# Products with the values issued three chunks at a time in a fused attention, experts and feed-forward kernel

## The chip, the cores and the metric

The kernel runs on one core of a Trainium2 chip. Its time is the device time of one execution in microseconds (us); three runs of the kernel before took 1173.31, 1173.35 and 1174.44 us, the median is 1173.35 us. The engines are TensorE (PE in the profile, its weight loads PEld), VectorE (DVE), ScalarE (ACT), GpSimd (POOL) and SyncE (SP), which here issues the transfers. Each engine works through its own instructions in their order, and waits at an instruction until the semaphores it names have come.

## The reference

The input passes three layers: attention whose queries are averaged in pairs, a mixture of eight experts of which each token takes one, and a dense feed-forward layer with softplus. All is float32. Only the attention is touched by the change in its order:

```python
def _attn_ref(q, k, v):                     # 4 batches, 8 heads, 1152 tokens, 64 wide
    q_pool = q.reshape(B, H, S // factor, factor, D).mean(axis=3)     # 576 queries
    scores = scale * np.matmul(q_pool, k.transpose(0, 1, 3, 2))
    scores = scores - np.max(scores, axis=-1, keepdims=True)
    attn = np.exp(scores)
    attn = attn / (np.sum(attn, axis=-1, keepdims=True) + 1e-09)
    return np.matmul(attn, v).astype(np.float32)
...
        h = np.maximum(x[mask] @ w1[e], 0.0)                 # experts, 512 -> 1024 -> 512
        out[mask] = gate_w[mask, None] * (h @ w2[e])
...
    h = x @ w_in                                             # 512 -> 2048 -> 512
    g = np.maximum(h, 0.0) + np.log1p(np.exp(-np.abs(h)))
    return (g @ w_out).astype(np.float32)
```

## The kernel before

The attention walks through 16 pairs of heads. A pair has two halves of 288 queries, a half has nine chunks of 128 keys, so there are 288 steps, numbered g; a step treats one chunk of keys for both heads of the pair. What one step issues stands in the loop of line 427:

- `smat(g+1)` (lines 163 to 169): the scores of the next chunk, keys on the partitions, four fp16 matmuls of 288 columns into one of two PSUM tiles `st`. The second of each two carries the low halves of the numbers and the row maximum, which was found earlier.
- `ex(g+1)` (line 170): ScalarE makes the exponentials of that chunk, float32, into a tile `P` (a ring of five buffers).
- `row` (line 421, `srow` in line 109): the scores are also computed the other way round, queries on the partitions, 384 keys at a time, only so that VectorE can take their maximum (line 121). That is done for a later pair, 27 rows a pair, and each row takes one of three PSUM tiles `sr`. `rows(g)` (line 334) says how many rows are to have been issued by step g: mostly five in three steps, and fewer for some twenty steps after each half batch, when VectorE has the routing of the experts to do.
- the events of the step (`ev`): loads, casts, the sums of the exponentials (`rsum`, line 188, in every ninth step), the routing (`lstage`, line 217). Many of these take an `sr` tile too. In a step rows and events take turns.
- `pv(g)` (line 207): the product of the exponentials of this chunk with the values, float32, one matmul for each head, 64 columns of weights each, the two side by side in the array and added up over the nine chunks in one PSUM tile `pv`. Each becomes two passes, so a `pv` is four records of line 212 in the trace.
- `add(g)` (line 174): GpSimd adds up the exponentials over groups of three chunks, for the sums.

At the end of a half `evac` copies the `pv` tile out on ScalarE. After the last step `tail` finishes the routing, then `moe_ffn` runs the experts and the feed-forward layer. The weights of the latter come as float64 words and are converted to float32 by VectorE (`convert`, line 981): twelve chunks during the attention, twenty during the experts. All 32 float32 chunks `W32` have a place in the pool `ws` from the start (line 934), 64 KB in each partition, and the fp16 low halves `wl` are written later into the same slots, each into that of the chunk before it (tags in lines 737 and 934).

The order on every engine is the order in which this code calls the instructions; no scheduler moves them.

Of the kernel before, what the change touches and what calls it, by code (L numbers as in the profile page):

```python
# [9 lines left out]
F32=mybir.dt.float32; F32R=mybir.dt.float32r; F16=mybir.dt.float16; I32=mybir.dt.int32; U32=mybir.dt.uint32  # L10
# [6 lines left out]
def attention(ctx,late,tc,I,C,x_dram,LG,gate,fill,early):  # L17
# [8 lines left out]
    rkp=late.enter_context(tc.tile_pool(name="rk",bufs=2,**R_))  # L26
    qsp=late.enter_context(tc.tile_pool(name="qs",bufs=1,**R_))
    vp=[late.enter_context(tc.tile_pool(name="v0",bufs=1,**R_)),ctx.enter_context(tc.tile_pool(name="v1",bufs=1))]
    pp=ctx.enter_context(tc.tile_pool(name="P",bufs=5))
    accp=ctx.enter_context(tc.tile_pool(name="acc",bufs=4)); ssp=ctx.enter_context(tc.tile_pool(name="ss",bufs=7))  # L30
    xup=ctx.enter_context(tc.tile_pool(name="xu",bufs=8))
    smp=ctx.enter_context(tc.tile_pool(name="sm",bufs=2))
# [127 lines left out]
    def dec(g):  # L160
        p,s=divmod(g,18); half,c=divmod(s,9)
        return p,half,c
    def smat(g):
        p,half,c=dec(g); ka,kb,q=KA[p%NS],KB[p%NS],Q[p%NS]
        st=stp.tile([128,2,512],F32,name="st"); ST[g]=st
        qs=slice(half*HQ,half*HQ+HQ); ks=slice(c*128,c*128+128)
        for h in range(2):
            nc.tensor.matmul(st[:,h,:HQ],lhsT=ka[:,h,ks],rhs=q[:,h,0,qs],start=True,stop=False)  # L168
            nc.tensor.matmul(st[:,h,:HQ],lhsT=kb[:,h,ks],rhs=q[:,h,1,qs],start=False,stop=True)  # L169
    def ex(g):  # L170
        P[g]=pp.tile([128,2,HQ],F32,name="P")
        nc.scalar.activation(out=P[g],in_=ST.pop(g)[:,:,:HQ],func=ACTF.Exp,scale=1.0/16)  # L172
    def groups(p,half): return (GL if half else GK) if p==NPAIR-1 else GS
    def add(g):

        p,half,c=dec(g)
        for n,G in enumerate(groups(p,half)):
            if c not in G: continue
            if len(G)==1: ACC[p,half,n]=P[g]
            if c==G[0]: return  # L180
            if c==G[1]: ACC[p,half,n]=accp.tile([128,2,HQ],F32,name="acc")
            A=ACC[p,half,n]
            B_=P[g-1] if c==G[1] else A
            if c in DVA.get(p,()): nc.vector.tensor_tensor(out=A,in0=B_,in1=P[g],op=ALU.add)
            else:
                for h in range(2): nc.gpsimd.tensor_tensor(out=A[:,h],in0=B_[:,h],in1=P[g][:,h],op=ALU.add)  # L186
# [20 lines left out]
    def pv(g):  # L207
        p,half,c=dec(g)
        if c==0: PV[p,half]=pvp.tile([128,512],F32,name="pv")
        t=PV[p,half]  # L210
        for h in range(2):
            nc.tensor.matmul(t[64*h:64*h+64,:HQ],lhsT=V[p][:,c,64*h:64*h+64],rhs=P[g][:,h],start=(c==0),stop=(c==NCH-1))  # L212
    def evac(p,half):
        XU[p,half]=xup.tile([128,HQ],F32,name="xu")
        nc.scalar.copy(out=XU[p,half],in_=PV.pop((p,half))[:,:HQ])  # L215
# [108 lines left out]
    NG=NPAIR*18; GS=((0,1,2),(3,4,5),(6,7,8)); GL=((0,1,2,3),(4,5,6),(7,),(8,)); GK=((0,1),(2,3),(4,5),(6,7,8)); ET=238; TS=(1,1,2,4,3); TX=(11,13); RSD=3; LD=2  # L324
# [4 lines left out]
    def dev(g):  # L329
        u=(g-64)%72  # L330
        return DV-u*DV/9 if u<18 else -DV+(u-18)*DV/27
    DV=4.5; FL=-0.6
    LC=dict(pe1=-1.7,pe2=-0.6,rb=0.22,lp=0.4,lr=0.4,ff=0.2,f=0.256)
    def rows(g): return min(NPAIR*SRN,R0+int((g+1)*2.65),int(55+1.65*(g-14)),int((g+1+LEAD)*1.5+dev(g)))
# [4 lines left out]
    def best(lo,hi):  # L339
        return min(range(lo,hi+1),key=lambda g:(round(busy[g],2),g))  # L340
# [17 lines left out]
    for lo,hi,(fa,*fs) in fill:  # L358
        lo=max(lo,last+1); hi=max(hi,lo+3); first=None
        for n,(f,c) in enumerate(zip(fs,(0.35,0.6,0.6))):  # L360
            g=best(lo,hi-2+n); lo=g+1
# [59 lines left out]
    def row(g):  # L421
        nonlocal done
        srow(done); done+=1
        if done%SRN==0:
            p=done//SRN-1; MF=mfin(p,5 if p==0 else 0); MF[0]()
            pend.extend([(g+d,f) for d,f in zip((1,1,1,1,1) if p==1 else (3,3,3,3,2),MF[1:])])
    for g in range(NG+1):
        if g+1<NG: smat(g+1)
        if g>=1 and g-1<NG:
            p,half,c=dec(g-1)  # L430
            if c==NCH-1: evac(p,half)
        if g+1<NG: ex(g+1)
        tgt=rows(g)
        es=ev.pop(g,[])
        while pend and pend[0][0]<=g: pend.pop(0)[1]()
        while done<tgt-(g<18) or es:
            if done<tgt-(g<18): row(g)
            if es: es.pop(0)()
        if g<NG: pv(g)
        while done<tgt: row(g)  # L440
        if g<NG: add(g)
    assert not [g for g in ev if ev[g]], sorted(ev)
# [147 lines left out]
class Kit:  # L590
# [15 lines left out]
    def three(s,o,wh_,wl_,x,first,last):  # L606
        nc=s.nc
        nc.tensor.matmul(o,lhsT=wh_,rhs=x[0],start=first,stop=False)  # L608
        nc.tensor.matmul(o,lhsT=wh_,rhs=x[1],start=False,stop=False)  # L609
        nc.tensor.matmul(o,lhsT=wl_,rhs=x[0],start=False,stop=last)  # L610
# [107 lines left out]
        for _ in range(n):  # L718
            if s.todo: s.K.unit(s.todo.pop(0))

def moe_ffn(ctx,mst,tc,I,C,Y,YE,wsp,W32,out,convert,ncv,K,P,bl):

# [2 lines left out]
    SP=[mybir.EngineType.SP]  # L727
    wip=ctx.enter_context(tc.tile_pool(name="wip",bufs=1,reuse_waits="tile"))
    WIH=wip.tile([128,4,DF],F16,name="WIH"); WOH=wip.tile([128,16,DM],F16,name="WOH")
    WL=[None]*32  # L730
    unit,lag,flush,three,reg=K.unit,K.lag,K.flush,K.three,K.reg
    def split(i):

        h=WIH[:,i%4,512*(i//4):512*(i//4)+512] if i<16 else WOH[:,i-16]
        f=SI if i<16 else SO
        nc.scalar.activation(out=h,in_=W32[i],func=ACTF.Copy,scale=f)
        WL[i]=wsp.tile([128,512],F16,name=f"wl_{i}",tag=f"ws{i}")
        nc.vector.scalar_tensor_tensor(out=WL[i],in0=W32[i],scalar=f,in1=h,op0=ALU.mult,op1=ALU.subtract)
    def WIL(k,f0): return WL[4*(f0//512)+k][:,f0%512:f0%512+128]
    def WOL(fc): return WL[16+fc]  # L740
    class Ffn:

        def __init__(s,n,x2,scat,P): s.n=n; s.x2=x2; s.scat=scat; s.P=P; s.g={}; s.m={}; s.e={}; s.hh={}; s.c=4//n; s.nu=16//s.c
        def F1(s,u,ks=range(4)):

            def f():
# [4 lines left out]
                for i in range(c):  # L751
                    f0=128*(c*u+i)
                    for k in ks:
                        three(h[:,i],WIH[:,k,f0:f0+128],WIL(k,f0),s.x2(k),k==0 and (i==0 or len(ks)==4),k==3 and (i==c-1 or len(ks)==4))
                if ks[-1]!=3: return
# [95 lines left out]
    while sp: split(sp.pop(0))  # L851
# [9 lines left out]
    P=dict(PC,**K.pools(tc,fst,[('xb','xb',1,0),('yr','yr',2,0),('io','fio',3,0),('tmp','tmp',2,0),('g','g',6,0),('po','po',1,1)]))  # L861
# [23 lines left out]
    with tc.For_i(0,nrem,1):  # L885
        with ExitStack() as st:
            P=K.pools(tc,st,[('raw','mraw',2,0),('hl','mhl',2,0),('io','io',2,0),('x','xx',2,0),('h','hT',1,0),('tmp','tmp',1,0),('g','g',4,0),('pl','pl',4,1),('pt','pt',1,1),('po','po',1,1)])
# [35 lines left out]
CH=((2,1),(3,1),(6,1),(7,1),(10,1),(11,1),(14,6))  # L923
P2ENG={mybir.EngineType.PE,mybir.EngineType.SP}
def tile_kernel(ctx,tc,I,out):
    nc=tc.nc
    if True:
      c1=ExitStack(); late=ExitStack(); mst=ExitStack(); P={}
      with tc.manual_schedule():
# [1 line left out]
        dp=ctx.enter_context(tc.tile_pool(name="dr",bufs=1,space=bass.MemoryType.DRAM))  # L931
        x_dram=dp.tile([2305,DM],F32,name="xs_dram"); Y=[dp.tile([128,2,YW],F32,name=f"y{k}_dram") for k in range(2)]; YE=[dp.tile([128,2,TB],F32,name=f"ye{k}_dram") for k in range(2)]
        wsp=ctx.enter_context(tc.tile_pool(name="ws",bufs=1))
        W32=[wsp.tile([128,512],F32,name=f"w32_{i}",tag=f"ws{i+1}") for i in range(32)]
        IDX=cp.tile([128,2*NB],I32,name="IDX"); IDS=cp.tile([128,2*NB],I32,name="IDS"); EV=cp.tile([128,NB+1],I32,name="EV")
        OFF=cp.tile([128,NBS],I32,name="OFF"); IDE=cp.tile([128,2],I32,name="IDE"); EVE=cp.tile([128,1],I32,name="EVE"); OFE=cp.tile([128,1],I32,name="OFE"); OE=cp.tile([128,8],F32,name="OE"); CIDS=cp.tile([128,2*NF],I32,name="CIDS"); cnt=cp.tile([128,8],F32,name="cnt"); RK=cp.tile([96,24],F32,name="RK"); OH=cp.tile([96,24,8],F16,name="OH")
        cc=cp.tile([128,496],F32,name="cc")
# [1 line left out]
        if True:  # L939
            q=c1.enter_context(tc.tile_pool(name="c1",bufs=1))  # L940
            C={}
# [3 lines left out]
            def t(n,s,d=F32):  # L945
                C[n]=q.tile(s,d,name=n); return C[n]
            id16=t('ident16',[128,128],F16); wgb=t('wgb',[128,4,32]); bias=t('bias',[96,24,8]); ones=t('ones16',[96,128],F16); tri=t('tri',[96,96],F16)
            t('RS',[96,9,8],F16); t('RB',[96,24]); t('OHID',[96,24,128],F16); C['EV']=EV; C['OFF']=OFF; C['CIDS']=CIDS; C['cnt']=cnt; C['RK']=RK; C['OH']=OH; C['IDE']=IDE; C['EVE']=EVE; C['OFE']=OFE; C['OE']=OE; C['IDX']=IDX; C['IDS']=IDS
            LG=t('LG',[96,24,8]); gate=t('gate',[96,24])
            bb=t('bb',[96,2,8]); md=t('md',[96,24,2],I32); mf=t('mf',[96,2,24]); bt=LG; zr=W32[31]  # L950
            def setup0():
                nc.vector.tensor_copy(out=ident,in_=cc[:,0:128])
                nc.vector.tensor_copy(out=id16,in_=cc[:,0:128])
# [27 lines left out]
            def convert(i,sg=sg,name="stg"):  # L981
# [3 lines left out]
                src=(I['w_in'][128*k:128*k+128,512*fb:512*fb+512] if i<16 else I['w_out'][128*(i-16):128*(i-16)+128])  # L985
                dst=W32[i].bitcast(I32)
                def a():
                    z['s']=sg.tile([128,512,2],I32,name=name) if name=="stg" else sg.tile([128,2,512],F32,name=name).bitcast(I32).rearrange("p a (n w) -> p (a n) w",w=2)
                    nc.sync.dma_start(out=z['s'].rearrange("p n w -> p (n w)"),in_=src.bitcast(I32))
# [4 lines left out]
            i=0  # L994
# [3 lines left out]
            K=Kit(nc,I,x_dram,ident)  # L998
            E=Early(K,tc,C,YE,P,mst)
            bl=[Moe(K,IDX[:,2*j:2*j+2],K.reg(EV[0:1,j:j+1],7),P) for j in range(NBS)]  # L1000
            tail=attention(c1,late,tc,I,C,x_dram,LG,gate,fill,E.schedule)
      ET=mybir.EngineType
      with tc.manual_schedule(engines=P2ENG):
        tail(E,bl[0])
        c1.close()
        with ExitStack() as c2:
            moe_ffn(c2,mst,tc,I,C,Y,YE,wsp,W32,out,convert,sum(n for _,n in CH),K,P,bl)
def lay(inp):
    A=np.ascontiguousarray
    q,k,v=inp['q'],inp['k'],inp['v']  # L1010
# [15 lines left out]
@with_exitstack  # L1026
def kernel(ctx: ExitStack, tc: tile.TileContext, arrays, out: bass.AP):
    tile_kernel(ctx, tc, arrays, out)
# [20 lines left out]
```

## Time and profile before

One execution was profiled: it took 1175.14 us, its recorded span is 1173.3 us, the granted clock of TensorE was 0.995 of full speed on the mean.

| | busy, us | share of the span |
|---|---|---|
| PE | 1113.8 | 95% |
| DVE | 869.0 | 74% |
| ACT | 646.2 | 55% |
| POOL | 499.7 | 43% |

The steps of the attention run from about 24 to 531 us. To read it: a matmul's record begins when the array takes it up and its end is modelled, so records overlap; what a matmul takes from the engine is the time from its start to the start of the next one, as long as none of them waits. In the timeline "x4" puts four records of one kind into one row, and square brackets give the idle time before an instruction and who ended it.

### The profile page before, as it was taken

What the parts mean: (1) busy time and instruction counts of PE and PEld (TensorE: products, weight loads), DVE (VectorE), ACT (ScalarE), POOL (GpSimd) and SP (SyncE); (2) the same over time, 40 slices, a digit from 0 to 9 for tenths busy, and PEclk for the clock granted to TensorE, in tenths of its full rate; (3) what the DMA queues carried; (4) which work ended last, traced back from release to release, by engine and by line L of the source; (5) the groups of instructions that cost most, each with busy time, mean ns of one, the idle gap of its engine ahead of it and who ended that gap; (6) DMA issues with size and microseconds to landing.
All of it is one profiled execution on the core that took longest, in us unless ns stands there. A gap on an engine that the chain in (4) does not pass through costs nothing. (4 is left out here: it accounts for less than half of the span.)

```text
span 1173.3 us, 20868 instructions
## 1 busy us (share of the span) xinstructions
PE 1113.8 (95%) x7887; PEld 625.0 (53%) x7887; DVE 869.0 (74%) x1583; ACT 646.2 (55%) x1096; POOL 499.7 (43%) x532
## 2 busy tenths in 40 slices
PE   5999999999999999999998898999999999999996
PEld 1444444444444444447777777887444444446663
DVE  5877697677867788858979788757977667767662
ACT  4666656666566655564755665655544444444441
POOL 7788876787678767472523332220000010100100
PEclk9999999999999999999999999999999999999999
DMA  9333417441453332233687777752100000000000
GB/s 243 79 82 108 118 49 197 120 117 31 125 149 95 96 82 77 74 130 119 213 284 260 276 259 272 242 176 77 36 19 27 18 18 19 28 9 11 36 10 30
DMA packets 42940, 129.48 MB, mean 110 GB/s; under 512 B 5841, under 2 KB 12881, under 8 KB 40914
## 3 DMA queue, kind: packets, MB, share of 16 engines
q1 hardware_dynamic: 39794, 118.12, 33.7%
q0 software_dynamic: 3040, 9.96, 2.5%
q8 instruction: 65, 1.06, 0.4%
q14 instruction: 41, 0.34, 0.1%
HBM read 108.13 MB, written 20.45 MB: 110 GB/s over the span
## 5 line engine op out<-in xcount | busy, mean ns | idle before, releaser
L121 DVE TENSOR_REDUCE mx<-sr 128x1 f32<-128x384 f32 x432 | 226.8, 550 | 108.0 <-PE sr L117 89.8
L172 ACT ACTIVATE P<-st 128x576 f32<-128x576 f32 x288 | 187.3, 650 | 171.6 <-PE st L169 159.5
L186 POOL TENSOR_TENSOR acc<-P 128x288 f32<-128x288 f32 x192 | 156.7, 837 | 116.7 <-ACT P L172 114.7
L212 PE MATMUL pv<-P,v 128*64 128x288 f32 x1152 | 203.8, 433 | 2.4 <-ACT xu L215 2.3
L793 POOL DMA_INDIRECT out_dram<-io,CIDS x18 | 21.1, 1174 | 358.5 <-ACT io L791 312.1
L168 PE MATMUL st<-Q,KA 128*128 128x288 f16 x576 | 157.1, 293 | 0.0
L169 PE MATMUL st<-Q,KB 128*128 128x288 f16 x576 | 154.3, 288 | 2.2 <-ACT Q L152 2.2
L186 POOL TENSOR_TENSOR acc<-acc,P 128x288 f32<-128x288 f32 x176 | 146.5, 853 | 6.5 <-ACT P L172 5.4
L117 PE MATMUL sr<-KA,Q 128*128 128x384 f16 x384 | 113.3, 335 | 13.6 <-ACT KA L90 8.2
L608 PE MATMUL l<-xf,WIH 128*128 128x256 f16 (+1 forms) x384 | 125.1, 326 | 0.9 <-ACT xf L814 0.9
L609 PE MATMUL l<-xf,WIH 128*128 128x256 f16 (+1 forms) x384 | 125.1, 326 | 0.2 <-DVE xf L815 0.2
L610 PE MATMUL l<-xf,wl 128*128 128x256 f16 (+1 forms) x384 | 125.1, 326 | 0.0
L168 PEld LDWEIGHTS <-KA 128*128 128x128 f16 x576 | 56.0, 97 | 128.6 <-issue 121.1
L645 ACT ACTIVATE mhl<-mraw 128x512 f16<-128x512 f32 x160 | 98.4, 625 | 47.0 <-PE l L610 19.1
L650 DVE SCALAR_TENSOR_TENSOR mhl<-mraw,mhl 128x512 f16<-128x512 f32 x140 | 96.5, 709 | 31.8 <-ACT mhl L645 31.4
L784 PE MATMUL o<-WOH,g 128*128 128x512 f16 x288 | 109.1, 379 | 0.9 <-DVE io L790 0.4
L786 PE MATMUL o<-WOH,g 128*128 128x512 f16 x288 | 109.1, 379 | 0.0
L785 PE MATMUL o<-wl,g 128*128 128x512 f16 x288 | 109.1, 379 | 0.0
L212 PEld LDWEIGHTS pv<-P,v 128*64 128x64 f32 x1152 | 59.4, 135 | 79.6 <-issue 42.0
L767 ACT ACTIVATE e<-e 128x1024 f32<-128x1024 f32 x36 | 38.0, 1057 | 101.4 <-DVE m L765 101.4
L609 PE MATMUL l<-hT,mhl 128*128 128x256 f16 x288 | 79.1, 275 | 6.6 <-DVE hT L677 6.6
L94 POOL TENSOR_TENSOR KB<-kr,KA 64x576 f16<-64x576 f32 x64 | 82.8, 1298 | 4.4 <-ACT KA L90 2.2
(246 smaller groups left out, 2164.2 us busy)
## 6 DMA issues: line engine op xcount, KB each, us to landing
mraw<-in_wm_dram SPq DMA_DIRECT2D x80, 512.0 KB, 4.7
kr<-in_k_dram SPq DMA_DIRECT2D x30, 576.0 KB, 10.2
qr<-in_q_dram SPq DMA_DIRECT2D x16, 576.0 KB, 7.4
v<-in_v_dram SPq DMA_DIRECT2D x16, 576.0 KB, 4.4
mraw<-in_w_out_dram SPq DMA_DIRECT2D x16, 512.0 KB, 5.0
stg<-in_w_in_dram SPq DMA_DIRECT2D x12, 512.0 KB, 4.4
y_dram<-w SPq DMA_DIRECT2D x20, 256.0 KB, 10.0
xs_dram<-xs SPq DMA_DIRECT2D x24, 192.0 KB, 2.1
```

Of the source, the lines that this page charges most:

```text
L117: nc.tensor.matmul(sr[:,:KW],lhsT=q[:,h,0,r0:r0+128],rhs=ka[:,h,k0:k0+KW],start=True,stop=True)
L121: nc.vector.tensor_reduce(out=MX[p][:,t,kh:kh+1],in_=sr[:,:KW],axis=AX.X,op=ALU.max,negate=True)
L168: nc.tensor.matmul(st[:,h,:HQ],lhsT=ka[:,h,ks],rhs=q[:,h,0,qs],start=True,stop=False)
L169: nc.tensor.matmul(st[:,h,:HQ],lhsT=kb[:,h,ks],rhs=q[:,h,1,qs],start=False,stop=True)
L172: nc.scalar.activation(out=P[g],in_=ST.pop(g)[:,:,:HQ],func=ACTF.Exp,scale=1.0/16)
L186: for h in range(2): nc.gpsimd.tensor_tensor(out=A[:,h],in0=B_[:,h],in1=P[g][:,h],op=ALU.add)
L212: nc.tensor.matmul(t[64*h:64*h+64,:HQ],lhsT=V[p][:,c,64*h:64*h+64],rhs=P[g][:,h],start=(c==0),stop=(c==NCH-1))
L608: nc.tensor.matmul(o,lhsT=wh_,rhs=x[0],start=first,stop=False)
L609: nc.tensor.matmul(o,lhsT=wh_,rhs=x[1],start=False,stop=False)
L610: nc.tensor.matmul(o,lhsT=wl_,rhs=x[0],start=False,stop=last)
L784: nc.tensor.matmul(o,lhsT=g[:,0,i,cs],rhs=WOH[:,fc],start=(fc==0),stop=False)
L785: nc.tensor.matmul(o,lhsT=g[:,0,i,cs],rhs=WOL(fc),start=False,stop=False)
```

## The change

Nothing that is computed changes. Three things move:

- The products with the values are issued only in every third step (g % 3 == 2), then for the chunks g-2, g-1 and g in a row. Nine chunks make a half, so each half has three such batches and there are 96 in all.
- From step 18 to step 247 the target of rows is one lower in the first two steps of three, so that one row moves from the first step of three to the third, ahead of the batch.
- The ring of `P` grows from five buffers to seven. For its place in SBUF the pool `ws` holds only the twelve chunks that are converted during the attention; the other twenty float32 chunks and all `wl` tiles get a pool of their own, opened when the attention's pools are closed. The zeros for the clearing of the output tables are made in chunk 11 instead of chunk 31.

```diff
-    pp=ctx.enter_context(tc.tile_pool(name="P",bufs=5))
+    pp=ctx.enter_context(tc.tile_pool(name="P",bufs=7))
...
-        tgt=rows(g)
+        c=g%3
+        tgt=rows(g)-((1,1,0)[c] if 18<=g<NG-40 else 0)
         es=ev.pop(g,[])
         while pend and pend[0][0]<=g: pend.pop(0)[1]()
         while done<tgt-(g<18) or es:
             if done<tgt-(g<18): row(g)
             if es: es.pop(0)()
-        if g<NG: pv(g)
+
+        if g<NG and c==2:
+            for k in (g-2,g-1,g): pv(k)
         while done<tgt: row(g)
         if g<NG: add(g)
...
+    wlp=ctx.enter_context(tc.tile_pool(name="wl",bufs=1,reuse_waits="tile"))
     WL=[None]*32
+    W32.extend(wlp.tile([128,512],F32,name=f"w32_{i}") for i in range(ncv,32))
...
-        WL[i]=wsp.tile([128,512],F16,name=f"wl_{i}",tag=f"ws{i}")
+        WL[i]=wlp.tile([128,512],F16,name=f"wl_{i}")
...
-        W32=[wsp.tile([128,512],F32,name=f"w32_{i}",tag=f"ws{i+1}") for i in range(32)]
+        NCA=sum(n for _,n in CH)
+        W32=[wsp.tile([128,512],F32,name=f"w32_{i}") for i in range(NCA)]
```

On PE, in the first half of pair 5, one step of the kernel before: a row (`sr`), the product of one chunk (`pv`), the scores of the next chunk (`st`), and again a row.

```order
L117 LDWEIGHTS Q0_195
L117 MATMUL sr_2450<-KA0_189,Q0_195 128x384
L212 MATMUL pv_2388<-P_2417,v_1956 64x288 x2
L168 LDWEIGHTS KA2_191
L168 MATMUL st_2457<-Q2_197,KA2_191 128x288
L169 LDWEIGHTS KB2_194
L169 MATMUL st_2457<-Q2_197,KB2_194 128x288
```

The same place now, the last step of three: two of its rows and then three chunks of exponentials (three tiles `P`), and only then the next scores.

```order
L117 LDWEIGHTS Q0_175
L117 MATMUL sr_2405<-KA0_169,Q0_175 128x384
L117 LDWEIGHTS Q0_175
L117 MATMUL sr_2410<-KA0_169,Q0_175 128x384
L212 MATMUL pv_2414<-P_2313,v_1931 64x288 x2
L212 MATMUL pv_2414<-P_2352,v_1931 64x288 x2
L212 MATMUL pv_2414<-P_2370,v_1931 64x288 x2
L168 LDWEIGHTS KA2_171
L168 MATMUL st_2423<-Q2_177,KA2_171 128x288
```

Three products stand together where one stood between a row and the scores, and the two others have gone from between the rows and scores ahead of them.

On PE behind such a place, before: the end of one chunk's scores, two rows, the product, the next chunk's scores.

```order
L169 MATMUL st_2391<-Q2_197,KB2_194 128x288
L117 LDWEIGHTS Q0_195
L117 MATMUL sr_2398<-KA0_189,Q0_195 128x384
L117 LDWEIGHTS Q0_195
L117 MATMUL sr_2402<-KA0_189,Q0_195 128x384
L212 MATMUL pv_2388<-P_2372,v_1956 64x288 x2
L168 LDWEIGHTS KA2_191
L168 MATMUL st_2412<-Q2_197,KA2_191 128x288
```

Now, right behind a batch: the scores of two chunks without anything between them.

```order
L168 LDWEIGHTS KA2_171
L168 MATMUL st_2423<-Q2_177,KA2_171 128x288
L169 LDWEIGHTS KB2_174
L169 MATMUL st_2423<-Q2_177,KB2_174 128x288
L168 LDWEIGHTS KA2_171
L168 MATMUL st_2432<-Q2_177,KA2_171 128x288
```

The first step of three has lost its row and its product, so the second `st` tile is filled directly behind the first. Counted over the whole order of the kernel now, with the rows in the first, second and third step of a batch: 48 batches hold 0, 2 and 3 rows (in two of them 0, 2 and 2), 16 hold 0, 1 and 2 (or 0, 1, 3; these are the stretches of the routing), 10 hold 1, 2 and 2 (one of them 1, 2, 1), 7 hold 1, 1 and 3, the first 6 hold up to 3 in every step, and the last 9 hold none.

## Rows read from the trace of the kernel before

**Rows 1.** Busy time of the engines in three stretches of the attention

```profile
core 0: us, PE busy (x) PEld busy (x) DVE busy (x) ACT busy (x) POOL busy (x), PEclk, DMA share, GB/s
24.40:530.60 506.20, 493.92 (x3707) 225.04 (x3708) 385.23 (x816) 310.24 (x554) 378.56 (x430) 1.00 0.38 104
156.00:192.00 36.00, 34.35 (x274) 17.13 (x274) 32.59 (x86) 20.02 (x39) 24.35 (x29) 1.00 0.37 103
192.00:254.00 62.00, 61.22 (x456) 27.20 (x456) 43.90 (x80) 40.80 (x72) 49.97 (x59) 1.00 0.46 125
```

**Rows 2.** What PE waited for, 60 to 540 us: total, times, longest

```profile
PE sr L117 <- DVE mx L121: 3.4, 5, 1.4
...
PE pv L212 <- ACT xu L215: 2.3, 10, 0.6
```

**Rows 3.** Timeline of two steps: start, duration, engine, line, operation

```profile
304.85 0.30 PE L168 MATMUL st<-Q,KA 128*128 128x288 f16 x1
...
305.23 0.29 PE L169 MATMUL st<-Q,KB 128*128 128x288 f16 x1
305.35 0.33 PE L117 MATMUL sr<-KA,Q 128*128 128x384 f16 x1
305.61 0.71 PE L212 MATMUL pv<-P,v 128*64 128x288 f32 x4
305.63 0.65 ACT L172 ACTIVATE P<-st 128x576 f32<-128x576 f32 x1 [2.54 <-PE st L169]
305.71 0.56 DVE L121 TENSOR_REDUCE mx<-sr 128x1 f32<-128x384 f32 x1 [0.54 <-PE sr L117]
...
306.25 0.30 PE L168 MATMUL st<-Q,KA 128*128 128x288 f16 x1
...
306.75 0.49 PE L117 MATMUL sr<-KA,Q 128*128 128x384 f16 x2
...
307.17 0.71 PE L212 MATMUL pv<-P,v 128*64 128x288 f32 x4
...
307.80 0.30 PE L168 MATMUL st<-Q,KA 128*128 128x288 f16 x1
```

**Rows 4.** Timeline of PE near the end of the attention

```profile
523.48 0.30 PE L168 MATMUL st<-Q,KA 128*128 128x288 f16 x1
...
524.71 0.30 PE L168 MATMUL st<-Q,KA 128*128 128x288 f16 x1
...
531.54 0.69 PE L197 MATMUL sr<-acc,one 128*32 128x288 f32 x8
532.05 0.67 PE L197 MATMUL sr<-P,one 128*32 128x288 f32 x8
532.65 0.28 PE L608 MATMUL sr<-xx,mhl 128*128 128x256 f16 x1
```

**Rows 5.** Timeline of PE and DVE early in the attention

```profile
28.68 0.34 PE L117 MATMUL sr<-KA,Q 128*128 128x384 f16 x1
28.85 0.29 PE L168 MATMUL st<-Q,KA 128*128 128x288 f16 x1
...
34.45 1.94 DVE L121 TENSOR_REDUCE mx<-sr 128x1 f32<-128x384 f32 x4
...
35.05 0.32 PE L117 MATMUL sr<-KA,Q 128*128 128x384 f16 x1 [0.55 <-DVE mx L121]
```

**Rows 6.** Groups of DVE by line, 60 to 480 us: busy, mean ns

```profile
L121 DVE TENSOR_REDUCE mx<-sr 128x1 f32<-128x384 f32 x362 | 191.0, 550 | 93.0 <-PE sr L117 75.9 <-PE sr L120 15.7
...
L132 DVE SCALAR_TENSOR_TENSOR nh<-nm,nh 128x9 f16<-128x9 f32 x13 | 8.8, 675 | 0.5
...
L131 DVE TENSOR_SCALAR nh<-nm 128x9 f16<-128x9 f32 x13 | 4.9, 379 | 0.5
...
L130 DVE TENSOR_REDUCE nm<-mx 128x9 f32<-128x27 f32 x13 | 2.4, 183 | 0.4
```

**Rows 7.** Exponentials (line 172): idle of ACT before them, by releaser

```profile
  POOL acc L186: 6.9, 9
```

More of the change, by code (lines that the diff above doesn't have):

```diff
@@ L719, in step, with moe_ffn @@
             if s.todo: s.K.unit(s.todo.pop(0))
-def moe_ffn(ctx,mst,tc,I,C,Y,YE,wsp,W32,out,convert,ncv,K,P,bl):
+def moe_ffn(ctx,mst,tc,I,C,Y,YE,W32,out,convert,ncv,K,P,bl):
     nc=tc.nc
@@ L949, in tile_kernel @@
             LG=t('LG',[96,24,8]); gate=t('gate',[96,24])
-            bb=t('bb',[96,2,8]); md=t('md',[96,24,2],I32); mf=t('mf',[96,2,24]); bt=LG; zr=W32[31]
+            bb=t('bb',[96,2,8]); md=t('md',[96,24,2],I32); mf=t('mf',[96,2,24]); bt=LG; zr=W32[NCA-1]
             def setup0():
@@ L1006, in tile_kernel @@
         with ExitStack() as c2:
-            moe_ffn(c2,mst,tc,I,C,Y,YE,wsp,W32,out,convert,sum(n for _,n in CH),K,P,bl)
+            moe_ffn(c2,mst,tc,I,C,Y,YE,W32,out,convert,NCA,K,P,bl)
 def lay(inp):
```

## The prediction

> **What bounds the kernel now.** I read the busy times by stretch first. Over the attention's steps PE is busy 493.92 of 506.20 us, DVE 385.23, POOL 378.56 and ACT 310.24 [rows 1]. The reader is to see that PE is the only engine without gaps. Then I read who PE waits for: over 480 us only 3.4 us for the row maxima and 2.3 us for the copy of the `pv` tile [rows 2]. So in this stage a microsecond that PE no longer needs is a microsecond of the kernel, as long as no other engine comes late. Third, the timeline gives what each step consists of [rows 3], from start to start:
>
> - scores of a chunk, to the next row: 305.35 - 304.85 = 0.50 us
> - a row before a product: 305.61 - 305.35 = 0.26; two rows: 307.17 - 306.75 = 0.42, so a row before a row takes 0.16
> - a product, to the next scores: 306.25 - 305.61 = 0.64
> - the step with one row 306.25 - 304.85 = 1.40, with two rows 307.80 - 306.25 = 1.55.
>
> A step of five rows in three takes 1.40 + 1.55 + 1.55 = 4.50 us for its three.
>
> **What is removed.** The product costs more than its own stream. A row before scores takes 28.85 - 28.68 = 0.17 us [rows 5], before a product 0.26: entering costs 0.09. How much less a product takes behind another product the trace does not show. The nearest rows are the sums of line 197, which are float32 too, 288 columns in two passes, and in another column tiling than the scores: one set of eight to the next set takes 532.05 - 531.54 = 0.51, the second set to an fp16 matmul 532.65 - 532.05 = 0.60 [rows 4]. So leaving costs about 0.09 as well, and 0.51 is my value for a product ahead of a product; the other end is 0.64, as now. A batch then takes 0.51 + 0.51 + 0.64 = 1.66 in place of 3 x 0.64 = 1.92, which saves 0.26, and two entries of 0.09 are gone: 0.44 us a batch, and 42 us over 96 batches, if nothing else comes late.
>
> The rows tie the 0.09 to the change of tiling only by their place: every such change in them is one of data type too. The Trainium skill, TensorEngine Tiling (Array Packing), Key Properties, says that changing the tiling mode, and not just the tile, drains the array. By that rule a product behind a product pays nothing, as I take it; the trace agrees with 0.51 against 0.60.
>
> **What comes late next.** Now a batch with 0, 2 and 3 rows (48 of 96), from the start of its first scores, each time by the intervals above. First scores at 0, second at 0.50, row a at 1.00, row b at 1.16, third scores at 1.33, rows c, d, e from 1.83, the last of them at 2.15.
>
> ACT: the second tile of scores follows at once, but the third needs the first `st` tile back. The exponential begins 305.63 - 305.23 = 0.40 after the last matmul of its scores and takes 0.65 [rows 3]; that matmul starts at 0.38, so it ends at 1.43. PE starts about 0.05 after a release (four reductions in 1.94 us with 0.55 for one: the first ends at 35.00, the row behind it starts at 35.05 [rows 5, 6]). So the third scores start at 1.48 instead of 1.33: 0.15 lost. Before, a product stood between any two scores and there was no such wait.
>
> DVE: there are three `sr` tiles, so row e needs the maximum of row b. A maximum starts 305.71 - 305.35 = 0.36 after its row [rows 3], takes 0.55, and the next one behind it starts (1.94 - 0.55) / 3 = 0.46 later [rows 5, 6]. That of row a starts at 1.36, of row b at 1.82 and ends at 2.37; row e at 2.42 instead of 2.15: 0.27 lost. The loss on ACT lies within it, since either way row e waits for b. So such a batch saves 0.44 - 0.27 = 0.17. In every third one the row sums (over 0.6 us of PE) stand between c and d; then only the 0.15 is lost and 0.29 is saved.
>
> With 1, 1 and 3 rows row b is early enough, and only ACT's 0.14 is lost: 0.30 saved. With 1, 2 and 2 rows nothing is late: 0.44 saved. In the routing stretches (16 batches) DVE is busy 32.59 of 36 us [rows 1], so a faster PE only waits more; the ends are 0 and 0.29, and I take 0.1, nearer to the end of a full engine. The first six batches have up to eight rows, which DVE needs 0.46 each for; ends 0 and 0.44, taken 0.1. The last nine have no rows. There a step takes 524.71 - 523.48 = 1.23 [rows 4], three 3.69; a batch 0.50 + 0.50 + 0.59 + 1.66 = 3.25, but the wait for ACT is 1.48 - 1.00 = 0.48: nothing is gained.
>
> **The sum**, in us:
>
> - 10 batches x 0.44 = 4.4; 7 x 0.30 = 2.1; 16 x 0.29 = 4.6; 32 x 0.17 = 5.4; 16 x 0.1 = 1.6; 6 x 0.1 = 0.6; 9 x 0
> - the wait for the copy of `pv`, 2.3 [rows 2], goes: the next product now comes three steps after the copy is issued
> - three times the end of a pair's maxima falls between rows a and b, and lines 130 to 132 take 0.18 + 0.38 + 0.68 = 1.24 on DVE ahead of b [rows 6]: -3.7.
>
> That is 17.3 us saved. Other DVE work (casts, conversions) mostly stands behind row b or behind the batch, where DVE has some 1.5 us without a row to look at; I price it at nothing, and at up to 0.5 a batch in the rival below.
>
> **What costs nothing.** The larger ring of `P`: a batch holds three tiles until its end, two more than before, and the ring has two more; ACT waited for POOL's sums only 6.9 us in all [rows 7], and its exponentials have slack outside the one chain above. The exponentials of a batch are there in time: the latest it needs comes from the second scores and is done by 1.43 + 0.65 = 2.08, and the batch begins after 2.6. The transfers keep their places among the steps, with PE's work and the waits on DMA as before. The float32 chunks: the twenty later ones are written during the experts, by the same instructions in the same place; the new pool lies where the attention's tiles were, whose last readers are done by then. No instruction is added there, and a wait on the chunk before, each in DVE's own order, goes. I take 0, and 1 us to either side.
>
> Against the profiled execution's own 1175.1 us this gives 1157.8. That execution lies 1.8 above the median of the runs, so I forecast 1156 us.
>
> **Rivals.**
>
> 1. The rings do not bind: the `st` and `sr` tiles come back sooner than in my chain, because records' ends are modelled. Then 87 batches (without the nine) save 0.44 and 2.3 goes: 40.6, so 1133 us. For it: PE waited for a maximum only five times. Against it: then there were never more than two rows and 0.64 us of product between any of them.
> 2. The change does not do what it says: a product behind a product still takes 0.64. Then only 0.18 a batch is saved, and with the same waits the classes give 10 x 0.18 + 7 x 0.04 + 16 x 0.03 - 32 x 0.09 + 2.3 - 3.7 = -1.7: 1175 us. For it: no row shows `pv` behind `pv`. Against it: 0.51 and 0.60 in line 197.
> 3. VectorE takes the place of PE and the kernel gets slower. Its place is row e, the last ahead of a batch: what waits there holds back the batch, the next scores and with them ACT and POOL. It decides when the maximum of row a starts more than 0.17 us later than 1.36, since the wait for e is then over 0.44. With 0.5 us of DVE's other work ahead of it, 48 batches lose 24 us more and the 16 of the routing 0.4 each, 6.4 more: 17.3 - 30.4 = -13, so 1187 us. For it: in the routing stretches DVE is at 90% already. Against it: in the others it is busy 43.90 of 62 us, 71% [rows 1], and has the batch to catch up. The Trainium skill, TensorEngine Tiling (Array Packing), PSUM Bottleneck, warns of just this: tiling speeds up the matmuls, not what empties PSUM. No row here shows it at the new pace.
>
> **How the numbers follow.** Forecast (most of the rings' cost, some gain left) 0.67, with its own range 1144 to 1168 us; rival 1 0.13; rival 2 0.05; rival 3 0.15. The bound of what can be told from no change is 0.2%, 2.3 us. Of the forecast's 0.67 some 0.07 lies within that bound, and rival 2 lies around it: faster 0.75, same 0.09, slower 0.16. The range reaches from rival 1's near side to where rival 3 begins, 1136 to 1177 us; I leave out 0.07 below and 0.12 above.
>
> **What would show it.** In the profile of the changed kernel: 12 records of line 212 in one row of the timeline, some 1.66 us to the next scores; the third scores of a batch waiting for `P` and its last row for `mx`; in the list of PE's waits these two in the place of 3.4 us, some 10 us or more together for the batches with three rows; the busy share of PE lower and the stretch of the steps some 17 us shorter, the experts and the feed-forward layer as long as before. I am wrong if the products in a batch are still 0.64 apart, if PE waits for `mx` over 30 us in total, or if the time changes behind the attention.

## The result and the profile after

Four runs of the changed kernel took 1187.9 to 1191.27 us, median 1190.53, beside 1173.89 for four of the kernel before: ratio 1.0125, 95% interval 1.0086 to 1.0164. The change made the kernel slower by about 17 us. Its profiled execution took 1191.27 us, with a span of 1189.5.

From the first scores of the first batch to those behind the last batch but one (the last has no scores behind it; my own difference of two starts in each trace) the kernel before took 503.8 us and the changed one 521.0, 17.2 more, so the whole loss lies in the attention. Its products with the values (line 212) did get cheaper on PE. That is in the page's list of groups (operation, count | busy, mean ns | idle before it); the same group before added up to 203.8 us:

```profile
L212 PE MATMUL pv<-P,v 128*64 128x288 f32 x1152 | 171.0, 435 | 0.0
```

First a batch where all went as forecast, in pair 5, with 0, 2 and 3 rows. The timeline of PE in the changed kernel (start, duration, engine, line, operation), which answers to [rows 3]:

```profile
201.23 0.30 PE L168 MATMUL st<-Q,KA 128*128 128x288 f16 x1
...
202.22 0.49 PE L117 MATMUL sr<-KA,Q 128*128 128x384 f16 x2
...
202.71 0.28 PE L168 MATMUL st<-Q,KA 128*128 128x288 f16 x1
...
203.20 0.78 PE L117 MATMUL sr<-KA,Q 128*128 128x384 f16 x3
...
203.91 1.68 PE L212 MATMUL pv<-P,v 128*64 128x288 f32 x12
...
205.52 0.30 PE L168 MATMUL st<-Q,KA 128*128 128x288 f16 x1
```

The batch of products takes 205.52 - 203.91 = 1.61 us, the third scores start at 202.71 - 201.23 = 1.48, and the period is 205.52 - 201.23 = 4.29 in place of 4.51, the same batch before: 0.22 saved.

Now the first routing stretch. The busy times by stretch, in the two traces between the same two batches' first scores (span us, busy of PE, PEld, DVE, ACT, POOL, granted clock, share and rate of DMA), answer to the second row of [rows 1]. Before:

```profile
153.21:177.89 24.68, 23.03 (x193) 11.47 (x191) 24.28 (x64) 14.79 (x28) 18.57 (x21) 1.00 0.28 75
```

After, and below it the other two routing stretches, which took 34.44 and 34.91 us before:

```profile
154.02:183.80 29.78, 24.82 (x192) 13.51 (x191) 25.92 (x65) 14.24 (x28) 17.77 (x20) 0.90 0.34 96
275.33:316.82 41.49, 35.60 (x267) 19.02 (x265) 32.92 (x80) 18.54 (x36) 25.27 (x28) 0.89 0.24 68
408.41:449.88 41.47, 35.54 (x267) 19.05 (x265) 32.90 (x80) 18.54 (x36) 25.27 (x28) 0.89 0.22 64
```

The same work takes 5.1, 7.1 and 6.6 us longer; PE, which had gaps of 1.65 us, now has 4.96, VectorE is busy 1.64 us longer with one instruction more in the window, and the granted clock is 0.90 and 0.89 in place of 1.00 and 0.99. The timeline of the changed kernel shows how these belong together:

```profile
163.97 1.27 POOL L94 TENSOR_TENSOR KB<-kr,KA 64x576 f16<-64x576 f32 x1
...
164.04 1.68 PE L212 MATMUL pv<-P,v 128*64 128x288 f32 x12
...
164.25 2.66 DVE L280 TENSOR_SCALAR r<-r,gate 96x8 f32<-96x8 f32 x3
...
165.21 1.53 POOL L186 TENSOR_TENSOR acc<-acc,P 128x288 f32<-128x288 f32 x2
...
166.82 0.55 DVE L121 TENSOR_REDUCE mx<-sr 128x1 f32<-128x384 f32 x1
...
167.16 1.54 POOL L186 TENSOR_TENSOR acc<-P 128x288 f32<-128x288 f32 x2 [0.42 <-ACT P L172]
...
167.29 2.19 DVE L307 TENSOR_SCALAR cm<-cc,RK 96x17 f32<-96x17 f32 x3
...
168.66 1.54 POOL L186 TENSOR_TENSOR acc<-acc,P 128x288 f32<-128x288 f32 x2
...
170.47 0.35 DVE L245 TENSOR_TENSOR lp<-sr,r 96x192 f32<-96x192 f32 x1
...
170.88 0.48 PE L117 MATMUL sr<-KA,Q 128*128 128x384 f16 x1 [2.32 <-DVE lp L245]
...
172.68 2.43 PE L212 MATMUL pv<-P,v 128*64 128x288 f32 x12
...
175.05 0.30 PE L168 MATMUL st<-Q,KA 128*128 128x288 f16 x1
...
175.86 0.40 ACT L215 COPY xu<-pv 128x288 f32<-128x288 f32 x1 [5.84 <-PE sr L285]
```

To read: line 280 multiplies eight columns by a number, three times, and line 307 compares 17 columns, three times. They take 2.66 and 2.19 us. In the kernel before, at the same place of the same stretch, POOL stands idle for 0.81 us from 165.40 on, and the same two rows of the timeline are:

```profile
165.25 0.50 DVE L280 TENSOR_SCALAR r<-r,gate 96x8 f32<-96x8 f32 x3
...
165.66 0.50 DVE L307 TENSOR_SCALAR cm<-cc,RK 96x17 f32<-96x17 f32 x3
```

In the changed kernel POOL meanwhile goes from one instruction to the next, with one gap of 0.42 us. Line 245, the last reader of an `sr` tile, stands behind both in VectorE's order, so PE waits 2.32 us for that tile. Then the granted clock is at its lower level, 1.2 of 2.4 GHz (0.50 from 171 to 174 us): a batch takes 175.05 - 172.68 = 2.37 instead of 1.61. ACT's copy of `pv`, which is next in ACT's order and needs this batch, comes after 5.84 us in which ACT stood idle. The changed kernel has nine such stretches of lower clock in the attention, eight of them in the routing; the kernel before has one.

By classes of batches, summed from start to start of the first scores behind each batch (us, after minus before; forecast beside it): the first six +2.5 (-0.6); ten with 1, 2, 2 rows -1.3 (-4.4); seven with 1, 1, 3 rows -1.3 (-2.1); 48 with 0, 2, 3 rows -1.5 (-10.0 and +3.7); nine without rows 0.0 (0); the 16 of the routing **+18.7** (-1.6). In each of the three stretches one to two batches carry most of it, with 2.7 to 4.4 us each.

### The profile page after: what moved, and what is told of

The parts are those of the page before. It is cut to its first block, busy times and chain, and to the rows that moved or that the text cites. A ratio compares the mean times of both kernels' runs of the same rounds, so it can differ in the third digit from the quotient of the medians.

```text
span 1189.5 us, 20861 instructions
## 1 busy us (share of the span) xinstructions
PE 1100.6 (93%) x7887; PEld 659.3 (55%) x7887; DVE 874.3 (74%) x1583; ACT 635.8 (53%) x1096; POOL 501.8 (42%) x532
## 5 line engine op out<-in xcount | busy, mean ns | idle before, releaser
L121 DVE TENSOR_REDUCE mx<-sr 128x1 f32<-128x384 f32 x432 | 222.8, 549 | 112.8 <-PE sr L117 91.1
L172 ACT ACTIVATE P<-st 128x576 f32<-128x576 f32 x288 | 181.8, 648 | 159.2 <-PE st L169 143.2
L212 PE MATMUL pv<-P,v 128*64 128x288 f32 x1152 | 171.0, 435 | 0.0
L168 PE MATMUL st<-Q,KA 128*128 128x288 f16 x576 | 154.4, 292 | 3.2 <-ACT P L172 2.8
L212 PEld LDWEIGHTS pv<-P,v 128*64 128x64 f32 x1152 | 78.6, 142 | 86.7 <-issue 51.5
```

Of the source, the lines that this page charges most:

```text
L121: nc.vector.tensor_reduce(out=MX[p][:,t,kh:kh+1],in_=sr[:,:KW],axis=AX.X,op=ALU.max,negate=True)
```

## The experiments

My theory, the port: behind a batch the exponentials come in a burst, GpSimd adds them up without a pause, and VectorE's short operations of the routing each wait one of its instructions out; so `sr` tiles come back late, PE stands idle, and its clock falls. The rival, the shift: it is the moved row that comes late, in the steady steps as in the routing. Beside them stand the new pools, and the question how much of the loss is the clock's.

Each ratio is to the kernel before on the same chip, with its 95% interval. "Routing" is the sum over the 16 routing batches, after minus before, counted as above.

**Pools alone**: products in every step and rows as before, so that the larger `P` ring and the later pool are left.

```diff
-        tgt=rows(g)-((1,1,0)[c] if 18<=g<NG-40 else 0)
+        tgt=rows(g)
-        if g<NG and c==2:
-            for k in (g-2,g-1,g): pv(k)
+        if g<NG: pv(g)
```

> Only the two pool edits: seven P buffers and the later pool for twenty float32 chunks; products in every step, no shift of rows. Theory port (in the routing stretches VectorE's short operations wait for GpSimd's sums, which come in bursts behind a batch): as before, 1172 to 1175 us. Theory shift (the row moved to the third step is what makes VectorE late): the same, 1172 to 1175. Theory pools (the new ring or the place of the chunks costs the time): 1185 to 1190.

1176.08 against 1176.83 us, 0.999 (0.9969 to 1.001). The two pools cost nothing that can be measured.

**Threes without the moved rows, and moved rows without threes**: the first line of the edit above alone, and the rest of it alone.

> The whole change without the shift of a row (1, 1, 0), so steady batches hold 1, 2 and 2 rows. Both theories: these 46 batches save about 0.5 us each against before instead of 0.2 to 0.35, some 11 us against the changed kernel. Theory shift: the 19 us lost in the routing stretches go as well, 1158 to 1164 us. Theory port: most of them stay, 1174 to 1182 us.

> The pools and the shift of rows alone, products in every step as before. Theory shift: the routing stretches are as long as in the changed kernel, 1185 to 1195 us. Theory port: GpSimd gets its exponentials at an even pace, the short operations wait no more than before, 1172 to 1179 us.

Without the moved rows: 1167.48, 0.9943 (0.9916 to 0.9969), routing +11.0. With the moved rows alone: 1183.69, 1.0066 (1.0033 to 1.0099), routing -0.4. Neither theory's totals hold; what both said of the steady batches, some 11 us, does (11.9 in the 48). Together they say: the routing's loss comes with the threes and needs no moved row, though the rows add to it; and in the 48 steady batches the moved rows alone cost 5.6 us, and with the threes 12 (-13.4 without them, -1.5 with them). There a batch with 1, 2 and 2 rows, in the timeline of the kernel without moved rows, takes 204.12 - 200.13 = 3.99 us:

```profile
200.13 0.30 PE L168 MATMUL st<-Q,KA 128*128 128x288 f16 x1
...
202.52 1.68 PE L212 MATMUL pv<-P,v 128*64 128x288 f32 x12
...
204.12 0.30 PE L168 MATMUL st<-Q,KA 128*128 128x288 f16 x1
```

That is 0.5 less than the 4.50 of before and 0.3 less than the 4.29 with rows moved.

**The routing as before**: the change everywhere but in the 16 routing batches.

```diff
+    RT=(24,25,26,27,46,47,48,49,50,51,70,71,72,73,74,75)
-        tgt=rows(g)-((1,1,0)[c] if 18<=g<NG-40 else 0)
+        nb=g//3 in RT; tgt=rows(g)-((1,1,0)[c] if 18<=g<NG-40 and not nb else 0)
+        if nb and g<NG: pv(g)
-        if g<NG and c==2:
+        if g<NG and c==2 and not nb:
```

> The whole change, but in the 16 batches of the three routing stretches products in every step and no shift, as before. Both theories: the loss is local, so the 18.7 us lost there go and the small gain elsewhere stays, 1169 to 1174 us. If the loss comes from anything outside those stretches it stays near 1190.

1170.28, 0.9965 (0.9946 to 0.9985), routing -0.8. The loss is local to these batches.

**Short operations taken together**: the changed kernel, with the four operations of the routing that run once per column group (lines 256, 266, 280, 307) as one `tensor_tensor` each over all three, the form that the last routing stage has already.

```diff
-            if last: V.tensor_tensor(out=z['r'].rearrange("p (t a) h -> p t (a h)",t=3),in0=z['r'].rearrange("p (t a) h -> p t (a h)",t=3),in1=e3(g),op=ALU.mult)
+            if True: V.tensor_tensor(out=z['r'].rearrange("p (t a) h -> p t (a h)",t=3),in0=z['r'].rearrange("p (t a) h -> p t (a h)",t=3),in1=e3(g),op=ALU.mult)
...
```

> The changed kernel with the routing's four threefold operations (lines 256, 266, 280, 307: one for each of three columns) made as one broadcast operation each. Theory port: each of the three waits for a GpSimd instruction of about 0.85 us, so the stretch loses up to 0.85 instead of 2.6 us at each of the four; of the 18.7 us lost in the routing stretches 10 or more go, 1174 to 1181 us. Theory latency (the batch of products on PE itself comes between the routing's transposes and VectorE, and what VectorE does in between does not matter): 1187 to 1192 us.

1165.31, 0.9893 (0.9868 to 0.9919): routing -6.0 in place of +18.7, more than expected. The first stretch in its trace:

```profile
156.36:179.47 23.11, 21.42 (x193) 12.40 (x191) 21.11 (x51) 14.12 (x28) 17.93 (x20) 1.00 0.35 100
```

In the groups of VectorE by line over the attention (busy, mean ns | idle) the four took 8.6 + 8.5 + 3.7 + 3.5 = 24.3 us in the kernel before:

```profile
L256 DVE TENSOR_SCALAR d<-LG,m 96x8 f32<-96x8 f32 x21 | 8.6, 465 | 0.0
...
L266 DVE TENSOR_SCALAR OH<-cc,f 96x8 f16<-96x8 f32 x21 | 8.5, 463 | 0.0
...
L280 DVE TENSOR_SCALAR r<-r,gate 96x8 f32<-96x8 f32 x21 | 3.7, 235 | 0.1
...
L307 DVE TENSOR_SCALAR cm<-cc,RK 96x17 f32<-96x17 f32 x21 | 3.5, 225 | 0.0
```

and in the changed kernel 5.7 + 12.8 + 12.3 + 8.5 = 39.3:

```profile
L266 DVE TENSOR_SCALAR OH<-cc,f 96x8 f16<-96x8 f32 x21 | 12.8, 665 | 0.0
...
L280 DVE TENSOR_SCALAR r<-r,gate 96x8 f32<-96x8 f32 x21 | 12.3, 640 | 0.1
...
L307 DVE TENSOR_SCALAR cm<-cc,RK 96x17 f32<-96x17 f32 x21 | 8.5, 461 | 0.0
...
L256 DVE TENSOR_SCALAR d<-LG,m 96x8 f32<-96x8 f32 x21 | 5.7, 329 | 0.0
```

With one operation for three they take 6.9 + 5.3 + 4.2 + 2.7 = 19.1:

```profile
L277 DVE TENSOR_TENSOR r<-r,gate 96x24 f32<-96x24 f32 x8 | 6.9, 868 | 0.1
...
L253 DVE TENSOR_TENSOR d<-LG,m 96x24 f32<-96x24 f32 x8 | 5.3, 665 | 0.1
...
L264 DVE TENSOR_TENSOR OH<-cc,f 96x24 f16<-96x24 f32 x8 | 4.2, 522 | 0.1
...
L304 DVE TENSOR_TENSOR cm<-RK,cc 96x51 f32<-96x51 f32 x8 | 2.7, 338 | 0.0
```

One such operation still waits (868 ns), but once and not three times. Two waits of ACT, which the change lengthened too, are as long as in the changed kernel: 12.7 us for GpSimd's sums in both (before: 6.9), and 36.7 against 35.0 for the products ahead of a copy of `pv` (before: 6.5; the three copies behind the stalls stand in another line of the list). So the loss did not hang on these two. And in the kernel before, the one for three:

> The kernel before with the same broadcast operations. Theory port: there the threefold operations waited little on the path, since PE had no wait behind them: 1168 to 1174 us, a gain well below that in the changed kernel. If a shorter chain of VectorE helps any order as much: 1160 us or less.

1168.56, 0.9924 (0.99 to 0.9949), routing -4.9. So by the ratios the same edit is worth 0.76%, 9 us, there, and 1.0125 - 0.9893 = 2.32%, 27 us, behind the change; the difference of 18 us is about what the change lost in the routing. With the one operation on both sides, the threes make the 16 routing batches 1.1 us shorter (-6.0 against -4.9) and not 18.7 longer.

**Fewer additions on GpSimd**: VectorE's instructions stay as in the changed kernel; in the 16 routing batches GpSimd's addition of each group's third chunk is left out, so the softmax sums lack those chunks.

```diff
+            if g//3 in RT and c==G[2]: return
```

> The changed kernel, but in the 16 routing batches GpSimd leaves out the second of its two additions in each group of three chunks, so the sums of the exponentials lack every third chunk there. VectorE's own instructions stay as they are. Theory port: GpSimd's share is halved there, a threefold operation meets an addition half as often, and of the 18.7 us lost in the stretches 8 or more go: 1172 to 1182 us. Theory number (what the broadcast operations cured was only the number of VectorE's instructions, not their wait for GpSimd): 1187 to 1192 us.

The total, 1300.01 (1.1031, 1.0968 to 1.1093), missed the expectation: with other weights other experts are chosen, and the loop over the experts runs longer (320 matmuls on each of its lines in place of 288). It says nothing of the change. In the attention, which that doesn't reach, routing is -4.1 in place of +18.7. Its first stretch, and below it VectorE's groups by line (two further down in this kernel: 258, 268, 282, 309):

```profile
151.29:174.55 23.26, 21.38 (x193) 12.39 (x191) 20.89 (x63) 14.10 (x28) 11.72 (x12) 1.00 0.33 93
```

```profile
L268 DVE TENSOR_SCALAR OH<-cc,f 96x8 f16<-96x8 f32 x21 | 8.9, 480 | 0.0
...
L282 DVE TENSOR_SCALAR r<-r,gate 96x8 f32<-96x8 f32 x21 | 7.8, 426 | 0.1
...
L258 DVE TENSOR_SCALAR d<-LG,m 96x8 f32<-96x8 f32 x21 | 4.3, 262 | 0.0
...
L309 DVE TENSOR_SCALAR cm<-cc,RK 96x17 f32<-96x17 f32 x21 | 3.5, 220 | 0.0
```

With POOL busy 11.72 instead of 17.77 us the same 21 comparisons of line 307 take 220 ns and not 461, without any edit to them. So what stretches them is GpSimd's work beside them. All four lines together take 24.5 us, as before the change. Over the runs their sum rises with the routing's loss: 24.8 us and -0.4 with the moved rows alone, 34.1 and +11.0 with the threes alone, 39.3 and +18.7 with both.

**Work for PE in its wait**: the changed kernel with twenty matmuls of 224 columns, whose result nobody reads, at three places in the routing, so that PE does not stand idle there.

```diff
+        if g in (80,152,224):
+            p,half,c=dec(g)
+            for _ in range(20): nc.tensor.matmul(PV[p,half][:,288:512],lhsT=KA[p%NS][:,0,:128],rhs=Q[p%NS][:,0,0,:224],start=False,stop=False)
```

> The changed kernel with twenty idle fp16 matmuls of 224 columns (about 0.09 us each) on PE at the place where it waits 2.3 us in each of the three routing stretches; their output is used by nothing. Theory clock (the granted clock falls there because PE waited, and this makes the next batch 0.8 us longer): the fall at 171 us and its two fellows go, the batch behind takes 1.6 again, 3 to 5 us less, 1185 to 1188 us. If the clock has another cause: 1190 us with the same falls, or more by what the matmuls take.

1182.78, 1.0041 (1.0022 to 1.0061); in the profiled execution (1188.5 us, the longest of ten) routing is +10.8. Its first stretch, and below it that stretch's timeline:

```profile
152.36:179.59 27.23, 24.03 (x213) 14.40 (x211) 25.63 (x63) 14.24 (x28) 17.80 (x20) 1.00 0.33 95
```

```profile
166.76 2.08 PE L431 MATMUL pv<-Q,KA 128*128 128x224 f16 x20
...
169.22 0.32 PE L117 MATMUL sr<-KA,Q 128*128 128x384 f16 x1 [0.38 <-DVE lp L245]
...
170.54 1.68 PE L212 MATMUL pv<-P,v 128*64 128x288 f32 x12
```

VectorE's operations are as late as before (line 280's mean is 619 ns), the row still waits for `lp`, but the clock is 1.00 and the next batch takes 1.61. Of the eight falls of the clock in the routing five are gone, and with them some 8 of the 18.7 us; by the ratios of the medians it is 1.0125 - 1.0041 = 0.84% or 10 us, with the two intervals 5 to 15, more than the 3 to 5 expected. The other 9 to 11 stay with the waits and with the three falls that are left in the second and third stretch.

**Both repairs**: threes and one operation for three, first without moved rows (as in the edit of the pools, its first line), then with rows moved only in batches 6 to 11 and in the routing.

```diff
+    SB=(6,7,8,9,10,11,24,25,26,27,46,47,48,49,50,51,70,71,72,73,74,75)
-        tgt=rows(g)-((1,1,0)[c] if 18<=g<NG-40 else 0)
+        tgt=rows(g)-((1,1,0)[c] if g//3 in SB else 0)
```

> The same broadcast operations in the changed kernel without the shift of a row. Theory port: of the 11 us that the routing stretches lose without the shift most go, 1156 to 1162 us. Theory latency: 1165 to 1170 us, as without the shift alone.

> A version put together from the runs: products three at a time, broadcast operations in the routing, and the shift of a row only in batches 6 to 11 and in the routing stretches, where the run without it was longer than the one with it by 2.5 and 3.5 us. By those two differences 1153 us, 1150 to 1157. If the parts don't add up, 1159 as without the shift.

1159.12, 0.9839 (0.9812 to 0.9865), and 1152.59, 0.9791 (0.9758 to 0.9824). The latter is faster than both kernels, and by the two ratios 16 us below the kernel before with the same four operations: that is what products in threes, with their rows placed so, are worth here.

## Why the prediction was wrong

**The step that failed** is the term for the routing stretches: "the ends are 0 and 0.29, I take 0.1". I read VectorE's 32.59 of 36 us [rows 1] as work of a fixed length, with which a faster PE could only wait more, so that nothing could get worse. The sum had no term for the clock either. The lengths are not fixed. In the changed kernel 20 of the 21 multiplications of line 280 began while a GpSimd instruction ran and took 0.66 us on the mean, the other one 0.22; before, 8 of 21 did, seven of them in its last 0.16 us, and the mean of all 21 was 0.235 (counted from the two traces). Of all 84 operations of the four lines 31 began beside a GpSimd instruction before, and 59 after. So each short operation that meets one waits it out, and the change made more of them meet. How it did so is not shown: my theory had GpSimd running longer without a pause, but in the three stretches GpSimd has nine runs of 4 us or more in the kernel before as well (up to 8.8 us, with gaps under 0.15 left out; nine after, up to 5.6). What moved is where VectorE's operations fall between GpSimd's instructions, and the runs tie that to the threes; the moved rows only add to it. The reductions of line 121 are not touched (550 ns before, 549 after), which is why the rows' own group gave no warning. From 1.6 us saved the term went to 18.7 lost, 20.3 of the 34.5 us between my sum and what the steps measured. Of that, the run with filler puts 8 to 10 us down to falls of the clock behind the waits.

The Trainium skill, SBUF — State Buffer, section "Who interferes with whom", says that VectorE and GpSimd share one pair of ports, that a `tensor_scalar` can enter a mode that uses it, that whoever issues first then holds it for its whole instruction, and that reductions never contend for it on trn2. The traces agree with 0.22 against 0.66 us for line 280 and 549 ns for the reduction; that it is this pair, no run here tells from another lock of the same effect. It was a rule that spoke against the change, and I did not weigh it.

**Rival 3** had the sign and, with 1187 us, nearly the size, but another place: row e of the steady batches. There PE has no wait to speak of: it is busy 59.02 of 60 us from 200 to 260 us. Of its price the 0.4 a batch for the routing was also far too small, and it knew nothing of the clock.

**Right, by measurement.** A product behind a product costs what I took (1.61 for the batch; 1.66 forecast), so rival 2 falls. The rings bind: third scores at 1.48 as worked out, row e no later, 0.22 saved where I had 0.17, and 0.35 where I had 0.29 with row sums; so rival 1 falls. What the moved row costs the 48 steady batches, by my chain 32 x 0.27 + 16 x 0.15 = 11.0 us and 3.7 with the ends of the maxima, measured 11.9 (-1.5 against -13.4 without it). With 1, 2 and 2 rows a batch takes 3.99 where nothing else is late (0.5 saved, 0.44 forecast). The end of a pair's maxima costs 1.4 to 1.5 a time (1.24 less 0.17 forecast), partly since its line 131 waits too, 1.25 us where it has 0.18 alone. PE's wait for the copy of `pv` (2.3 us) is gone from its list of waits. The pools cost nothing. Nothing changed behind the attention.

**Sizes that were off beside it.** The 48 steady batches gave 1.5 us, not 6.3: the typical one agrees, but three batches ahead of the first routing stretch and one behind each of the first two are 0.2 to 0.7 longer, beside the three with the ends of maxima. The forecast took 2.3 us off for the copy of `pv` on top of the classes; in the measured sums that is within them. The ten with 1, 2 and 2 rows gave 1.3 and not 4.4; why the six early ones gain only 0.2 wasn't settled by a run. The first six lost 2.5 in this execution, where the clock fell once at 34 us. No row moves there, and in the profiled executions without the moved rows and with the filler, the same instructions without that fall, they gained 0.5, which is the -0.6 of the forecast.

**The bound I gave** for being wrong, over 30 us of PE waiting for `mx`, was the wrong sign to look for. In the list of PE's waits over the attention (total, times, longest), which answers to [rows 2] (in the kernel before over the same window 4.2, none, 2.4 and 1.0):

```profile
PE sr L117 <- DVE mx L121: 13.5, 20, 1.7
PE sr L117 <- DVE lp L245: 6.9, 3, 2.3
PE sr L296 <- DVE mx L121: 4.2, 3, 1.7
PE sr L296 <- DVE OH L266: 2.9, 5, 1.3
```

Three waits of 2.3 us for `lp`, one in each routing stretch, started most of the loss; the list shows what PE waited for and not what the lower clock then took.

## What to carry to other kernels

Before issuing work of one engine in bursts, ask what it moves on the others: here a new order on PE brought VectorE's shortest operations beside GpSimd's instructions, and those set how long they took. An engine at 90% is no harmless floor if the durations of its instructions depend on a neighbour: look for a line whose mean is a multiple of its fastest instance. One broadcast operation in place of three small ones pays twice then, since each of the three waits by itself.

## What the runs showed of the hardware

- An operation of 0.22 us on VectorE took 0.83 us where it waited out one of GpSimd's additions, and up to 1.79 us where two of GpSimd's instructions followed each other (three operations in 2.66 us); the four lines took 39.3 us instead of 24.3 before the change.
- The clock cost about as much as the waits that came before its falls: behind 2.32 us in which PE waited, the granted clock stood at its lower level, and the stretch's two batches at that level took 2.37 and 2.92 us instead of 1.61. Filling one wait in each stretch with matmuls that nobody reads took away both falls of the first stretch and five of eight in all, and 8 to 10 us.
- Moving one row in five cost 5.6 us in the 48 steady batches even with the products left where they were, though no work was added. In that run's trace 33 of the 48 are as long as before; the longest loss, 1.32 us in one batch, goes with a wait of 1.16 us of PE for a row maximum. The other causes weren't tried.
